# Half-precision expert operands, doubled attention buffers, routing tables in pieces, and a new order for the first pairs

## The chip, the core and the metric

One core of a Trainium2 chip runs the whole program. The time is the device time in microseconds. Three runs of the kernel before took 1328.16 to 1332.0 us, median 1330.05 us. All the views of the profile come from one profiled execution of 1328.04 us.

## The reference

Two stages, both in float32. The first is attention over 64 heads (8 batches of 8), 1152 keys of 64 numbers each, with queries averaged in twos, so 576 query rows per head:

```python
q_pool = q.reshape(B, H, S // factor, factor, D).mean(axis=3)
scores = scale * np.matmul(q_pool, k.transpose(0, 1, 3, 2))
scores = scores - np.max(scores, axis=-1, keepdims=True)
attn = np.exp(scores)
attn = attn / (np.sum(attn, axis=-1, keepdims=True) + 1e-09)
return np.matmul(attn, v)
```

Its output becomes 4608 tokens of 512 numbers. The second stage gives each token to one of 8 experts: all 4608 x 8 logits are walked in descending order, a pair is taken if its token is still free and its expert has fewer than 576 tokens, so every expert ends with exactly 576. Then, for each expert, two layers:

```python
h = np.maximum(x[mask] @ w1[e], 0.0)   # 512 -> 1024
out[mask] = h @ w2[e]                  # 1024 -> 512
```

## The kernel before

**Precision.** TensorE (PE) multiplies in pairs: an operand is split into a high part and a low part (what the high part leaves), and a product is the sum of three (high x high, high x low, low x high). In the attention the parts are half precision, with a power of two per head pair as scale (`SC`), which comes from a bound on the sums over K, Q and V (`bounds`). In the experts high and low parts are float32 tiles that PE reads in its rounded float32 form (`FR`).

**Attention.** 32 head pairs, n = 0 to 31; each pair is 18 steps g: two heads times nine blocks of 128 keys. A step makes scores (PE, `sc`, two f16 products), the exponential (ACT, `P`, 576 columns), a low part of it (POOL or DVE, `PM`), and the product with V (PE, `av`). For the next pair the same time holds the exact row maxima (PE into `ma` and `mb`, DVE reduces them into `MX`), the bounds and scales (ACT sums absolute values into `VM` with `accum_out`, line 439), the split of K, Q and V into f16 parts (`KH`, `KL`, `QH`, `QL`, V's parts), and SP's copies of these into `KA`, `KB`, `QA`, `QB` (`spread`). The loads are `KD`, `QD`, `VD`, issued by SP for the next pair. Of `KD`, `QD`, `VD`, `QS` (the summed queries), `KL` and `QL` there is one buffer each; `KH`, `QH` and others have two.

What sets the order there is the class `Cycle`: every operation carries a tag and a number, and a table (`TAU`; `TAU0` for what is added with pair 0's preparation, `TAU1` for that of pair 1) gives it a place in a period of 25 units. A heap takes, among those whose inputs have been planned, the one with the smallest place. Each engine then runs its operations strictly in that order: an operation that waits holds all behind it on its engine. Before the first pair PE runs `wu` + `wv` = 52 filler matmuls.

**Routing tables.** `routing_tables` makes constants for the routing: POOL writes number rows, and three blocks of DVE operations (`order`, `digits`, `places`, lines 293 to 320) make tables of them. All carry the tag `tab` with base 2, so that they fall beside pairs 2 and 3.

**Experts.** The first `route` takes the best tokens of expert 0, alone; each later expert's routing runs beside the layers of the one before, in rounds of small steps: PE (`rt`), DVE, PE, DVE. `fetch` then gathers, from POOL, the tokens (`XG`, in five indirect transfers of up to 128 rows) and the weights (`W`), and splits them: the high part is a copy by ACT, the low part a subtraction by POOL or DVE. `ffn` runs layer one (`ph`: 8 blocks f times two halves of the tokens, 256 and 320 columns, 12 matmuls each), a relu on ACT and its low part on DVE (`HX` holds both, 2 x 576 columns), and layer two (`po`: five column blocks c of tokens, four with 128 tokens and 24 matmuls of 512 columns each; c = 4 has the last 64 tokens: 8 matmuls of 128 rows, which hold the high and the low part, and 8 of 64 rows with `W2L`). The results (`OT`) go out by POOL's indirect transfers. All the split tiles (`W1H`, `W1L`, `W2H`, `W2L`, `XH`, `XL`) have one buffer.

The class `Order` plans this part: each operation has an earliest time, a duration and a priority (`first`), a transfer the time it is expected to take (`late`), and per engine the one that can start first goes next. The weight splits are written W1, W2, W1, W2 and so on by quarter z. For experts from 2 on, tokens come transposed by SP (`by_dve`): XL is two subtractions on POOL and two on DVE.

## Time and profile before

| what | us |
|---|---|
| median of three runs | 1330.05 |
| profiled execution | 1328.04 |
| its span | 1326.1 |
| first exponential (pair 0) | 24.7 |
| pair 0, to the first exponential of pair 1 | 54.3 |
| pair 3 | 31.9 |
| pairs 4 to 30, together (157.31 to 785.70) | 628.4 |
| pair 31 and the tail of the attention (to 810.25) | 24.6 |
| routing of expert 0 (to 850.30) | 40.1 |
| experts 0 to 4, with the routing of the next (to 1161.46) | 311.2 |
| experts 5 to 7 (to 1314.45) | 153.0 |
| tail (to 1326.10) | 11.7 |

Times are in microseconds from the start of the span, names of tiles are the program's, and a line number is that of the kernel before. PE is the matmul side of TensorE and PEld its weight loads, which overlap with it; DVE is VectorE, ACT ScalarE, POOL GpSimd, SP the engine that issues most transfers. `PEclk` is the granted clock of TensorE. In a timeline a row gives start, duration, engine, line and operation, and in brackets the time that the engine stood idle before, with what released it.

### The profile page before, as it was taken

What the parts mean: (1) busy time and instruction counts of PE and PEld (TensorE: products, weight loads), DVE (VectorE), ACT (ScalarE), POOL (GpSimd) and SP (SyncE); (2) the same over time, 40 slices, a digit from 0 to 9 for tenths busy, and PEclk for the clock granted to TensorE, in tenths of its full rate; (3) what the DMA queues carried; (4) which work ended last, traced back from release to release, by engine and by line L of the source; (5) the groups of instructions that cost most, each with busy time, mean ns of one, the idle gap of its engine ahead of it and who ended that gap; (6) DMA issues with size and microseconds to landing.
All of it is one profiled execution on the core that took longest, in us unless ns stands there. A gap on an engine that the chain in (4) does not pass through costs nothing.

```text
span 1326.1 us, 38213 instructions
## 1 busy us (share of the span) xinstructions
PE 1264.2 (95%) x15398; PEld 1008.8 (76%) x15398; DVE 1035.6 (78%) x2619; ACT 803.7 (61%) x1423; POOL 907.0 (68%) x831
## 2 busy tenths in 40 slices
...
PEclk8599999999999999999999998999999999999998
...
GB/s 166 99 138 172 100 144 173 147 143 167 156 157 136 175 149 140 173 156 156 139 168 150 105 45 19 163 14 187 171 103 176 114 142 162 159 112 169 89 13 36
DMA packets 123533, 175.19 MB, mean 132 GB/s; under 512 B 49500, under 2 KB 86364, under 8 KB 121180
## 3 DMA queue, kind: packets, MB, share of 16 engines
...
q8 instruction: 121, 1.98, 0.6%
...
q10 hardware_dynamic: 144, 0.02, 0.0%
...
## 4 chain that ended last, share of the span: by engine, by line
PE 74%; DVE 19%; issue 3%; ACT 1%; DMA 1%; POOL 1%; POOLq 0%; DVEq 0%; ACTq 0%
PE sc L656 17%; PE ph L1374 15%; PE av L673 14%; PE po L1404 13%; DVE MX L576 5%; PE ma L573 4%; PE mb L573 4%; DVE KL L515 2%; DVE PM L663 1%; PE av L708 1%; PE rt L1052 1%; DVE MX L585 1%; DVE ST L1170 1%; PE av L796 1%; PE av L720 1%
## 5 line engine op out<-in xcount | busy, mean ns | idle before, releaser
L663 POOL TENSOR_TENSOR PM<-P 128x576 f16<-128x576 f32 x504 | 612.6, 1242 | 161.2 <-PE av L673 86.9
L659 ACT ACTIVATE P<-sc,EX 128x576 f32<-128x576 f32 x576 | 408.2, 739 | 128.6 <-PE sc L656 118.7
L673 PEld LDWEIGHTS <-P 128*128 128x128 bf16 x5760 | 299.9, 98 | 31.9 <-issue 1.6
L673 PE MATMUL av<-V,P 128*128 128x65 f16 (+1 forms) x5760 | 311.3, 193 | 0.1
L673 PE MATMUL av<-V,PM 128*128 128x65 f16 x2880 | 301.3, 195 | 0.8 <-POOL PM L663 0.8
L673 PEld LDWEIGHTS <-PM 128*128 128x128 f16 x2880 | 265.9, 97 | 1.0 <-POOL PM L663 1.0
L656 PE MATMUL sc<-QB,KB 65*128 65x288 f16 (+1 forms) x1152 | 239.4, 289 | 0.0
L656 PE MATMUL sc<-QA,KA 128*128 128x288 f16 x1152 | 238.2, 288 | 1.2 <-ACT P L659 1.2
L576 DVE TENSOR_REDUCE MX<-ma 128x1 f32<-128x512 f32 x279 | 190.0, 681 | 16.1 <-PE ma L573 11.6
L576 DVE TENSOR_REDUCE MX<-mb 128x1 f32<-128x512 f32 x279 | 190.4, 683 | 4.6 <-PE mb L573 2.6
L656 PEld LDWEIGHTS <-KA 128*128 128x128 f16 x1152 | 104.3, 97 | 80.3 <-issue 33.5
L1404 PE MATMUL po<-W2H,HX 128*128 128x512 f32 x512 | 164.8, 397 | 0.0
L1374 PE MATMUL ph<-XL,W1H 128*128 128x320 f32 (+1 forms) x512 | 155.5, 304 | 1.3 <-DVE XL L1307 1.3
L1374 PE MATMUL ph<-XH,W1H 128*128 128x320 f32 (+1 forms) x512 | 155.1, 303 | 0.9 <-DVE XL L1273 0.9
L1374 PE MATMUL ph<-XH,W1L 128*128 128x320 f32 (+1 forms) x512 | 154.9, 303 | 0.0
L1379 ACT ACTIVATE HX<-ph 128x320 fp32r<-128x320 f32 (+1 forms) x128 | 52.5, 410 | 147.6 <-PE ph L1374 140.9
L656 PEld LDWEIGHTS <-KB 65*128 65x128 f16 (+1 forms) x1152 | 113.9, 99 | 31.1
L1404 PE MATMUL po<-W2L,HX 128*128 128x512 f32 (+1 forms) x320 | 126.7, 396 | 0.0
L573 PE MATMUL mb<-KH,BD 128*128 128x512 f16 x279 | 108.2, 388 | 9.1 <-DVE MX L576 6.8
L573 PE MATMUL ma<-KH,BD 128*128 128x512 f16 x279 | 107.7, 386 | 9.5 <-DVE MX L576 5.8
L1418 POOL DMA_INDIRECT out_dram<-OT,idx x40 | 39.4, 984 | 109.8 <-ACT OT L1409 83.8
L1404 PEld LDWEIGHTS po<-W2H,HX 128*128 128x128 f32 x512 | 95.0, 188 | 17.8
...
## 6 DMA issues: line engine op xcount, KB each, us to landing
...
QA<-QH SPq DMA_DIRECT2D x128, 72.0 KB
...
```

The source lines that it names most:

```text
L515: fn=lambda h=h: nc.vector.scalar_tensor_tensor(KL[0][:, h], KD[0][:, h], KS, KH[i][:, h], op0=OP.mult, op1=OP.subtract),
L573: od.add(t, "PE", 214, lambda: nc.tensor.matmul(m, BD[i][:, j, :], KH[i][:, 512 * c:512 * c + 512], start=True, stop=True), r=bd + [("KH", ...
L576: od.add(t, "DVE", 597, lambda: nc.vector.tensor_reduce(MX[i][:, j, c:c + 1], m, axis=AX.X, op=OP.max), r=[mk], w=[("MX", i, j, c)], tag=" ...
L585: od.add(t, "DVE", 64 + 133 * len(js), lambda: nc.vector.tensor_reduce(MX[i][:, j:j + len(js), 2], m[:, :128 * len(js)].rearrange("p (a b) ...
L656: nc.tensor.matmul(c[:, t, :288], a[i][:rows, s, ks], b[i][:rows, s, 288 * t:288 * t + 288], start=first, stop=not first)
L659: od.add(g + 0.1, "ACT", 624, lambda: nc.scalar.activation(p.rearrange("p (t q) -> p t q", t=2), c[:, :, :288], AF.Exp, scale=EX[n % 3][:, ...
L663: od.add(g + 0.2, en, dur, lock=1, fn=lambda: eng.tensor_tensor(pm, p, hi, op=OP.subtract), r=[("P32", g % NP)], w=[("PM", g % NM)], tag="pm")
L673: nc.tensor.matmul(out, w[:, qs], v, start=kb == 0 and j == 0 and y == 0, stop=kb == NKB - 1 and y == 2, skip_group_check=True)
L1374: nc.tensor.matmul(p, a[:, d, fs], b[:, d, qs], start=z == 0, stop=z == 11)
L1379: nc.scalar.activation(HH[:, f, qs], p, AF.Relu)
L1404: nc.tensor.matmul(o[:n], a[:, z, q0:q0 + n], b[:, z], start=z == 0 and y == 0, stop=z == 7, skip_group_check=True)
L1418: st = nc.gpsimd.indirect_dma_start(out=out, out_offset=bass.IndirectOffsetOnAxis(ap=idx[i][:n, c:c + 1], axis=0), in_=OT[ob][:n], in_offs ...
```

## The change

In the experts all operands become half-precision pairs. So that they fit its range, x, W1 and W2 are multiplied by powers of two, and the result by their inverse product. The scale of x comes from the sums of squares of V: ACT's bound on V is now a Square instead of an absolute value, with the sums kept in `VQ`. The scale of W1 comes from all of W1: during the attention SP reads it in 32 pieces of 512 KB, one per pair (`weights`, into the one buffer `WB`), and ACT sums each piece's squares. `last_scale` forms both scales in the last pair (`SX`). The scale of W2 comes per expert from four Squares over 1024 columns on ACT, four small PE sums and five small DVE operations (`squares`: `SW`, `IT`). The split is now a scaled copy by ACT into the f16 high part, a second scaled copy by ACT in place, and POOL's subtraction. (Expert 0's first quarter of W1 takes one DVE operation in place of the last two.) As f16 tiles are half as large, each of W1H, W1L, W2H, W2L, XH and XL now has two buffers. W1 is split whole before W2. XL is four or five DVE operations of 128 elements per partition for each of four groups, 18 in all, for experts from 2 on. The first two experts read W1 in halves, no longer behind any token index.

For c = 4 of layer two the 64-row matmuls with W2L come in pairs, one into the lower and one into the upper 64 rows of the output (column tiles).

In the attention `KD`, `QD`, `VD`, `QS`, `KL` and `QL` have two buffers. Pairs 1 and 2 have tables of their own (`TAU1`, `TAU2`), pair 0's steps use `TAU0`, and all numbers of the tables are new; PE gets 16 + 18 more fillers (`wx`, `wy`). V's scale is a DVE operation (`halved`) and an ACT operation of its own. The routing tables are 16 pieces, one per pair from pair 4 on, and POOL's number rows are spread from pair 2 on.

```diff
-            l = (TAU, TAU0, TAU1)[zero][tag]
+            l = (TAU, TAU0, TAU1, TAU2)[zero][tag]
...
+       -130.9575], "ldv": [-89.6074], "ldw": [-1.436], "me": [-20.3883, -10.8961, -7.8442], "mm": [-27.6499, -27.3342,
...
+       [-38.3162, -42.8418], "vsh": [-36.7156], "wsq": [10.2686], "x": [-190.5431, 1.6364]}
...
-AT = {"load": -14.1, "vload": -13.6, "split": -10.3, "bound": -10.3, "bq": 0.1, "bv": -0.1, "bs": 0.1, "spread": 2.0,
...
+AT = {"load": -10.5, "vload": -15.2, "split": -10.3, "bound": -10.3, "bq": 0.1, "bv": -0.1, "bs": 0.1, "spread": 2.0,
+      "val": -5.6, "vh": -1.4, "vd": -0.5, "mm": -3.9, "cw": 0.737, "fold0": 3.5, "fold1": 11.3, "aug": 12.8, "lag":
+      6, "np": 10, "nm": 10, "stick": 1, "nx": 3, "wu": 30, "pd": [4, 12], "wv": 22, "pd0": [], "pd1": [3, 5, 6, 7, 9,
+      10, 11, 12, 13, 16], "d1": 2.0, "cw1": 0.7, "wx": 16, "wy": 18}
...
+    for dur, fn in pieces:
+        do("DVE", dur, fn)
...
-    KL = several(1, [128, S], F16, "KL")
+    KL = several(2, [128, S], F16, "KL")
...
-    KD = several(1, [128, S], F32, "KD")
-    QD = several(1, [128, 2, M], F32, "QD")
-    VD = several(1, [128, 2, NKB, D], F32, "VD")
-    QS = several(1, [128, M], F32, "QS")
+    KD = several(2, [128, S], F32, "KD")
+    QD = several(2, [128, 2, M], F32, "QD")
+    VD = several(2, [128, 2, NKB, D], F32, "VD")
+    QS = several(2, [128, M], F32, "QS")
...
+    def weights(n, t):
+        e, z = divmod(n, 4)
+        od.add(t, "SP", 650, lambda: nc.sync.dma_start(WB, w1[128 * e:128 * e + 128, 1024 * z:1024 * z + 1024]), w=["WB"],
+               tag="ldw", late=6500)
+        od.add(t, "ACT", 1030, lambda: nc.scalar.activation(VJ[:, :1024], WB, AF.Square, accum_out=WQ[:, n:n + 1]),
+               r=["WB"], w=[("WQ", n)], tag="wsq")
...
+        def put():
+            nc.vector.tensor_copy(WM[:, 0:1], mb[:, 128:129])
+            nc.vector.tensor_reduce(WM[:, 1:2], mb[:, 136:144], axis=AX.X, op=OP.max)
+            nc.vector.tensor_scalar(XE, WM.bitcast(I32), 0x7F800000, 0x7F800000, op0=OP.bitwise_and, op1=OP.bitwise_xor)
+            nc.vector.tensor_scalar(XE, XE, 1, 0x7F800000, op0=OP.arith_shift_right, op1=OP.bitwise_and)
+            f = XE.bitcast(F32)
+            nc.vector.tensor_scalar(SX[:, 0:1], f[:, 0:1], 2.0 ** 73, None, op0=OP.mult)
+            nc.vector.tensor_scalar(SX[:, 2:3], f[:, 1:2], 2.0 ** 67, None, op0=OP.mult)
+            nc.vector.scalar_tensor_tensor(SX[:, 1:2], SX[:, 2:3], 2.0, SX[:, 0:1], op0=OP.mult, op1=OP.mult)
+
+        od.add(t, "PE", 110, lambda: nc.tensor.transpose(mb[:32, :128], VQ, ident), r=[("VQ", n) for n in range(npair)], w=["mb"], tag="sx")
+        od.add(t, "DVE", 200, lambda: nc.vector.tensor_reduce(VR, mb[:32, :128], axis=AX.X, op=OP.max), r=["mb"], w=["VR"], tag="sx")
+        od.add(t, "PE", 60, lambda: nc.tensor.matmul(mb[:, 128:129], ones[:32], VR, start=True, stop=True), r=["VR"], w=["mb"], tag="sx")
+        od.add(t, "PE", 110, w_sums, r=[("WQ", n) for n in range(npair)], w=["mb"], tag="sx")
...
-                    VJ[:, :src.shape[1]], src, AF.Abs, accum_out=VM[i][:, c:c + 1]), r=rd, w=[("VM", i, c)], tag="abs")
+                    VJ[:, :src.shape[1]], src, AF.Abs if c < 2 else AF.Square,
+                    accum_out=VM[i][:, c:c + 1] if c < 2 else VQ[:, n:n + 1]), r=rd, w=[("VM", i, c)] + [("VQ", n)] * (c == 2), tag="abs")
...
+        def halved():
+            nc.vector.tensor_scalar(e[:, 1, 2:3], e[:, 1, 2:3], 1, 0x7F800000, op0=OP.arith_shift_right, op1=OP.bitwise_and)
...
-        for _ in range(AT[x]):
-            od.add(-70, "PE", 213, lambda: nc.tensor.matmul(av[1], ones, wide, start=True, stop=True), w=["av1"], tag=x)
+    for x, t, b in (("wu", -70, 1), ("wv", -70, 1), ("wx", -45, 0), ("wy", 20, 0)):
+        for _ in range(AT.get(x, 0)):
+            od.add(t, "PE", 213, lambda b=b: nc.tensor.matmul(av[b], ones, wide, start=True, stop=True), w=[f"av{b}"], tag=x)
...
+        if not g % NSTEP:
+            weights(g // NSTEP, g)
...
+
+    def table(eng, dur, fn):
+        pools.append(eng == "POOL")
+        od.base = max(4, od.base + 1) if eng == "DVE" else 2 + sum(pools) // 4
+        od.add(NSTEP * (od.base + 1), eng, dur, fn, w=["tables"], lock=True,
+               tag="tab" if eng == "DVE" else "tap")
...
-    W1H, W1L = one([128, 4, F], FR, "W1H"), one([128, 4, F], FR, "W1L")
-    W2H, W2L = one([128, 8, DM], FR, "W2H"), one([128, 8, DM], FR, "W2L")
+    W1H, W1L = ([one([128, 4, F], F16, f"W1{x}{b}") for b in range(2)] for x in "HL")
+    W2H, W2L = ([one([128, 8, DM], F16, f"W2{x}{b}") for b in range(2)] for x in "HL")
+    SX = C["SX"]
+    SQ = one([128, 1024], BF, "SQ")
+    WQ = [one([128, 4], F32, f"WQ{b}") for b in range(2)]
+    WE = one([128, 1], I32, "WE")
+    SW = [one([128, 1], F32, f"SW{b}") for b in range(2)]
+    IT = [one([128, 2], F32, f"IT{b}") for b in range(2)]
...
-    XH, XL = one([128, 4, CAP], FR, "XH"), one([128, 4, CAP], FR, "XL")
-
-    HX = one([128, 8, 2 * CAP], FR, "HX")
+    XH, XL = ([one([128, 4, CAP], F16, f"X{x}{b}") for b in range(2)] for x in "HL")
+
+    HX = one([128, 8, 2 * CAP], F16, "HX")
...
+            def low(src=src, s=s, nc_=nc_):
+                for c in range(nc_):
+                    q = slice(128 * c + 32 * s, 128 * c + 32 * s + 32)
+                    V.scalar_tensor_tensor(XL[k % 2][:, :, q], src[:, :, c], SX[:, 0:1], XH[k % 2][:, :, q], op0=OP.mult, op1=OP.subtract)
...
+            od.add(t + 0.35, "DVE", 190 * nc_, low, r=xf + xg + hk, w=lk, first=LT["ft"])
...
-        if k:
+        if k > 1:
             od.add(t, "POOL", 1300, weight(W1.rearrange("p a b c -> p (a b c)"), w1), r=[("widx", i)], w=[("W1", 0), ("W1", 1)],
-                   late=LT["w"])
+                   late=LT["w"], first=LT["fp"])
         else:
             for h in range(2):
                 od.add(t + 0.15 * h, "POOL", 1100, weight(W1[:, h].rearrange("p b c -> p (b c)"),
-                       w1.rearrange("r (h x) -> (r h) x", h=2), widx2[:, h:h + 1]), r=["widx2"] + [("idx", i, c) for c in range(5 * h)], w=[("W1", h)], late=LT["w0"])
+                       w1.rearrange("r (h x) -> (r h) x", h=2), widx2[:, h:h + 1]), r=["widx2"], w=[("W1", h)], late=LT["w0"], first=LT["fp"])
...
-        for z in range(4):
-            for nm in ("W1", "W2"):
...
+        b = k % 2
+        squares(k, t + 0.6)
+        for nm in ("W1", "W2"):
+            for z in range(4):
...
+                    od.add(tt, "ACT", 475, lambda o=hi[p], a=raw[p], w=w: nc.scalar.activation(o, a, AF.Copy, scale=w),
+                           r=[key] + wk, w=[hk], first=first)
+                    if k or z > LT["zd"] or nm == "W2":
+                        od.add(tt, "ACT", 475, lambda a=raw[p], w=w: nc.scalar.activation(a, a, AF.Copy, scale=w),
+                               r=[key, hk] + wk, w=[sk], first=first)
+                        od.add(tt, "POOL", 1230, lambda o=lo[p], a=raw[p], h=hi[p]: nc.gpsimd.tensor_tensor(
+                            o, a, h, op=OP.subtract), r=[key, hk, sk], w=[(nm + "L", b, z, y)], first=first, late=LT["lw"])
...
+        for z in range(4):
+            od.add(t, "ACT", 1030, lambda z=z: nc.scalar.activation(
+                SQ, raw[:, 1024 * z:1024 * z + 1024], AF.Square, accum_out=WQ[b][:, z:z + 1]), r=["W2"], w=[qk[z]], first=first)
...
+            if c < 4:
+                for z in range(8):
+                    for y, (a, b) in enumerate(((HH, W2H), (HH, W2L), (HL, W2H))):
+                        def mm2(c=c, o=o, z=z, y=y, a=a, b=b[bb]):
                             q0 = 128 * c + (64 if a is HL else 0)
-                            nc.tensor.matmul(o[:n], a[:, z, q0:q0 + n], b[:, z], start=z == 0 and y == 0, stop=z == 7,
+                            nc.tensor.matmul(o, a[:, z, q0:q0 + 128], b[:, z], start=z == 0 and y == 0, stop=z == 7 and y == 2)
+                        od.add(t + 0.7, "PE", 214, mm2, r=hkeys(z), w=[("po", c % 2)])
...
+                for z in range(0, 8, 2):
+                    for y in range(2):
+                        od.add(t + 0.7, "PE", 214, lambda o=o, z=z + y: nc.tensor.matmul(
+                            o, HX[:, z, 512:640], W2H[bb][:, z], start=z == 0, stop=False, skip_group_check=True),
+                            r=hkeys(z + y), w=[("po", c % 2)])
+
+                    def halves(o=o, z=z):
+                        for y in range(2):
+                            nc.tensor.matmul(o[64 * y:64 * y + 64], HH[:, z + y, 512:], W2L[bb][:, z + y], start=False, stop=z == 6,
                                              skip_group_check=True)
```

**ACT, second head of pair 0.** `P` is an exponential of pair 0; `VJ` with `VM0` are the sums over pair 2's QS, KD and VD, `QH1` and `KH1` the splits of pair 1. Before:

```order
L439 ACTIVATE VJ_123,VM1_122<-VD0_119 128x1152
L462 ACTIVATE SC1_112<-VE1_125 128x3
L500 ACTIVATE QH1_89<-QS0_120,SC1_112 128x576
L512 ACTIVATE KH1_86<-KD0_117,SC1_112 128x576
L466 ACTIVATE EX1_115<-SC1_112 128x1
L467 ACTIVATE EX1_115<-VE1_125 128x1
L547 ACTIVATE V161_102<-VD0_119,SC1_112 128x9x64 x2
L439 ACTIVATE VJ_123,VM0_121<-QS0_120 128x576
L512 ACTIVATE KH1_86<-KD0_117,SC1_112 128x576
L439 ACTIVATE VJ_123,VM0_121<-KD0_117 128x1152
L439 ACTIVATE VJ_123,VM0_121<-VD0_119 128x1152
L659 ACTIVATE P320_129<-sc0_155,EX0_114 128x576
```

With the change, around the same sums:

```order
L741 ACTIVATE P322_143<-sc0_167,EX0_116 128x576
L507 ACTIVATE VJ_135,VM0_127<-QS0_125 128x576
L741 ACTIVATE P324_145<-sc0_167,EX0_116 128x576
L741 ACTIVATE P323_144<-sc1_168,EX0_116 128x576
L741 ACTIVATE P325_146<-sc1_168,EX0_116 128x576
L507 ACTIVATE VJ_135,VQ_129<-VD0_123 128x1152
L741 ACTIVATE P327_148<-sc1_168,EX0_116 128x576
L507 ACTIVATE VJ_135,VM0_127<-KD0_119 128x1152
L741 ACTIVATE P326_147<-sc0_167,EX0_116 128x576
```

The sums over pair 2's data stood in one block with pair 1's splits, ahead of the exponentials; now single exponentials of pair 0 stand between and before them.

**PE, last column block of an expert** (`HX` holds the activations, `W2H` and `W2L` the weights). Before:

```order
L1401 MATMUL po_16006<-W2H,HX 128x512
L1404 MATMUL po_16006<-W2L,HX 64x512
L1401 MATMUL po_16006<-W2H,HX 128x512
L1404 MATMUL po_16006<-W2L,HX 64x512
```

With the change:

```order
L1549 LDWEIGHTS HX
L1549 MATMUL po_16239<-W2H_16211,HX 128x512
L1549 LDWEIGHTS HX
L1549 MATMUL po_16239<-W2H_16211,HX 128x512
L1555 LDWEIGHTS HX
L1555 MATMUL po_16239<-W2L_16213,HX 64x512
L1555 LDWEIGHTS HX
L1555 MATMUL po_16239<-W2L_16213,HX 64x512
```

The 64-row matmuls now come two by two, behind two of 128 rows; their two outputs are the two halves of the same tile.

**POOL, fetch of the first expert** (`W` raw weights, first both halves of W1, then W2; `XG` the tokens). Before:

```order
L1317 DMA W_15986<-in_w_dram,widx_15977 128x2048
L1322 DMA XG<-x_dram,idx_15969 128x512 x4
L1322 DMA XG<-x_dram,idx_15969 64x512
L1317 DMA W_15986<-in_w_dram,widx_15977 128x2048
L1317 DMA W_15987<-in_w_dram,widx_15978 128x4096
L1357 TENSOR_TENSOR W1L<-W_15986,W1H 128x2x256 x6
```

With the change:

```order
L1419 DMA W_16205<-in_w_dram,widx_16196 128x2048 x2
L1424 DMA XG<-x_dram,idx_16188 128x512 x4
L1465 TENSOR_TENSOR W1L_16209<-W_16205,W1H_16207 128x2x256
L1424 DMA XG<-x_dram,idx_16188 64x512
L1419 DMA W_16206<-in_w_dram,widx_16197 128x4096
L1465 TENSOR_TENSOR W1L_16209<-W_16205,W1H_16207 128x2x256 x5
```

Both halves of W1 now go ahead of the tokens, and the last token transfer stands behind a subtraction.

333 lines of the change are left out of this document (187 added, 146 removed), and 90 rows, old and new, of tables (AT, TAU, TAU0, TAU1).

## The prediction

> **What bounds the kernel now.** I read the page first, then the busy time in stretches, then the chain of waits in the stretches that lose most. The page:
>
> ```profile
> PE 1264.2 (95%) x15398; PEld 1008.8 (76%) x15398; DVE 1035.6 (78%) x2619; ACT 803.7 (61%) x1423; POOL 907.0 (68%) x831
> PE 74%; DVE 19%; issue 3%; ACT 1%; DMA 1%; POOL 1%; POOLq 0%; DVEq 0%; ACTq 0%
> PEclk8599999999999999999999998999999999999998
> ```
>
> PE (TensorE) carries the end, except in the second slice, where the granted clock is half. The stretches (columns: start and end, length, then busy us of PE, weight loads, DVE, ACT, POOL, then granted clock, DMA share, GB/s) are pair 0, pair 3, twelve steady pairs, the first expert's routing, expert 0, the gap behind it, experts 1 to 4, and experts 5 to 7:
>
> ```profile
> 24.70:78.98 54.28, 44.10 (x334) 22.59 (x334) 37.35 (x69) 28.21 (x49) 19.70 (x17) 0.59 0.42 113
> 125.42:157.31 31.89, 24.53 (x387) 19.03 (x388) 29.82 (x68) 19.73 (x34) 20.39 (x19) 0.89 0.42 104
> 227.36:506.64 279.28, 277.13 (x4566) 218.30 (x4563) 267.93 (x501) 237.79 (x404) 234.61 (x193) 1.00 0.60 155
> 810.25:850.30 40.05, 31.30 (x242) 20.40 (x242) 31.00 (x154) 3.50 (x7) 7.37 (x8) 0.87 0.18 58
> 850.30:909.46 59.16, 59.16 (x402) 49.76 (x400) 44.68 (x191) 20.75 (x44) 29.31 (x30) 1.00 0.40 151
> 909.46:916.01 6.55, 3.48 (x29) 2.37 (x27) 5.53 (x15) 6.50 (x13) 6.34 (x8) 1.00 0.42 131
> 916.01:1161.23 245.22, 237.62 (x1591) 202.02 (x1592) 184.08 (x762) 79.74 (x171) 153.21 (x158) 0.98 0.43 140
> 1161.46:1314.45 152.99, 152.99 (x913) 138.40 (x911) 34.39 (x85) 51.12 (x110) 80.82 (x86) 1.00 0.28 88
> ```
>
> A steady pair is 279.28/12 = 23.27 us; PE is busy for 99% of it, DVE idles 0.95 us and ACT 3.46. Pair 0 takes 31.0 more than that, pair 3 8.6 more. An expert without routing beside it takes 152.99/3 = 51.0 us; the first five with the gap took 310.9, which is 55.9 over 5 x 51.0.
>
> **Pair 0.** ACT's timeline, the PE row of the scores that its exponentials wait for, and the chain of waits there:
>
> ```profile
> 47.60 0.76 ACT L512 ACTIVATE KH<-KD,SC 128x576 f16<-128x576 f32 x1
> 59.38 1.16 ACT L439 ACTIVATE VJ<-KD 128x1152 bf16<-128x1152 f32 x1 [11.02 <-DMA KD<-in_kt_dram]
> 60.66 1.16 ACT L439 ACTIVATE VJ<-VD 128x1152 bf16<-128x1152 f32 x1
> 61.73 0.19 ACT L439 ACTIVATION_READ_ACCUMULATOR VJ<-VD 128x1 f32 x1
> 61.82 0.72 ACT L659 ACTIVATE P<-sc,EX 128x576 f32<-128x576 f32 x1
> ```
> ```profile
> 44.43 0.68 PE L656 MATMUL sc<-QB,KB 69*128 69x288 f16 x2
> ```
> ```profile
> 51.32 7.97 DMA KD<-in_kt_dram
> ```
>
> Scores of pair 0's second head lie ready at 45.1, but the next exponential in ACT's order stands behind a sum over pair 2's KD; with one KD buffer that load waits until pair 1 has read it. ACT stands 11.02 us, and PE has little to do in that time and half a clock. With two buffers the load goes long before, and the new order puts the exponentials ahead of that sum. At least the 7.97 us of the chain goes; at most all of DVE's idle time in the pair, 54.28 - 37.35 = 16.9, because its maxima for pair 1 remain. What is late next is those maxima, at half clock. I take -12, between the two; ends -17 and -3, if the exponentials then collide with pair 1's maxima. The 34 new filler matmuls of 512 columns (16 ahead of pair 0's first exponentials, 18 behind its last) take 0.215 each by the attention's rows below, 7.3 in all, and double at half clock. DVE is what pair 0 follows, so they lie in PE's waits: 0; with that cover gone they cost 7 to 15, and if they bring the full clock sooner, they give a few back. Both stay inside the ends of this term, since I know no row that says where the clock would turn.
>
> **Tables.** The routing tables' three blocks on DVE:
>
> ```profile
> 126.59 0.56 DVE L293 TENSOR_SCALAR before<-jp 128x128 bf16<-128x128 int32 x1
> 129.43 1.04 DVE L297 CAST pcol<-scratch 128x2 f32<-128x2 int32 x1
> 134.70 0.68 DVE L576 TENSOR_REDUCE MX<-mb 128x1 f32<-128x512 f32 x1
> ```
>
> From 126.59 to 134.70 DVE does no maxima: 8.1 us, nearly all of pair 3's 8.6. The 16 pieces go to pairs with 0.95 us of DVE idle time each. Some operations there are long for their size (1.04 for two columns), so the sum of the pieces is under 8.1. I take -7.5; ends -8.6 and -4 (half of it on the path again).
>
> **Steady pairs.** New per pair: on DVE one tiny operation (bound 0.19, the accumulator read above is as small), on ACT a Square over 1024 columns (under the 1.16 + 0.19 of the 1152 above) and a second small scale, together some 1.5, on PE one small matmul, on SP one 512 KB load. DVE's 0.95 and ACT's 3.46 idle cover them; uncovered DVE work costs 31 x 0.19 = 6. The table of places is new throughout, which only a run can price: PE has 279.28 - 277.13 = 2.15 us of idle time in twelve pairs, so it can gain 5 over all at most. Taken +3, ends -4 and +12. The scale of x at the end has nine tiny DVE operations and a few PE steps, 2 us if bare, but it is wanted only when the first expert's tokens come, at the end of the 40.05 us of routing: 0.
>
> **First expert's fetch.** POOL's issue, ACT's first cast and the first expert matmul:
>
> ```profile
> 842.22 0.95 POOL L1322 DMA_INDIRECT XG<-x_dram,idx  x1 [1.30 <-DVE ixf L1179]
> ```
> ```profile
> 845.76 2.18 ACT L1354 CAST W1H<-W 128x512 fp32r<-128x512 f32 x4 [35.26 <-DMA W<-in_w_dram,widx]
> ```
> ```profile
> 850.30 0.36 PE L1374 MATMUL ph<-XH,W1H 128*128 128x256 f32 x1
> ```
>
> Now both halves of W1 are issued ahead of the token gathers: one issue more (0.95 + 0.3 between issues), and the last gather stands behind a subtraction that waits for weights and ACT. It can be hidden (the first cast then also comes earlier for half 1). +2, ends 0 and +4.
>
> **Experts, PE.** The chain beside the routing of expert 1, and in the last experts:
>
> ```profile
> 865.39 2.28 PE ph L1374 x17
> 867.67 0.27 PE rt L1052 x5
> 867.93 1.36 PE ph L1374 x8
> 869.29 0.02 PE rt L1062
> 869.32 2.56 PE ph L1374 x19
> ```
> ```profile
> 1161.62 25.59 PE ph L1374 x192
> 1187.21 21.79 PE po L1404 x96
> ```
>
> ph takes 25.59/192 = 0.1333 (a mean of 256 and 320 columns), po 21.79/96 = 0.227; the last 16 of 51.0 are the fifth column at the same 0.227. What half precision takes is in the attention (start to start):
>
> ```profile
> 139.81 0.38 PE L573 MATMUL mb<-KH,BD 128*128 128x512 f16 x1
> 140.02 0.41 PE L656 MATMUL sc<-QA,KA 128*128 128x288 f16 x2
> 140.26 0.41 PE L656 MATMUL sc<-QB,KB 65*128 65x288 f16 x2
> 140.51 0.38 PE L573 MATMUL ma<-KH,BD 128*128 128x512 f16 x1
> ```
>
> 512 columns 0.215, 288 columns 0.122 (by ratio 0.1357 for 320, 0.1086 for 256). An expert: 192 x 0.122 = 23.4; 96 + 8 full ones x 0.215 = 22.4; four pairs of tiles at about 0.223 = 0.9 if a pair runs together. 46.7, or -4.3 for each of eight: -34.
>
> Whether tiles run together:
>
> ```profile
> L720 PE MATMUL av<-XT,wgs x6: 485/488/489, 119.0 to 119.4; 128*8 128x384 f32 x6
> ```
>
> Six matmuls of 384 columns started within 0.4 us, while one alone would take 0.227 x 384/512 = 0.17: they overlap. But a return from small tiles may cost: after the five rt above, 8 ph took 1.36 instead of 1.07. At 0.29, four returns in eight experts cost 9, more than the 8 x 4 x 0.21 = 7 that the tiles save. The Trainium skill's page "TensorEngine Tiling (Array Packing)" says under Key Properties that changing the tiling mode drains the TensorE, and under Restrictions that column tiling disables Fast Weight Load; both speak against this part, and the slow stretch after rt agrees, though a wait could make it too. By that rule the tiles would give back what they save.
>
> **Experts, the rest.** Per expert ACT does 16 more in-place scalings and four Squares. Casts and relus beside experts 1 to 4:
>
> ```profile
> L1354 ACT CAST W1H<-W 128x512 fp32r<-128x512 f32 x32 | 17.9, 618 | 0.0
> L1379 ACT ACTIVATE HX<-ph 128x256 fp32r<-128x256 f32 (+1 forms) x64 | 26.3, 410 | 88.6 <-PE ph L1374 83.8 <-PE rt L1062 4.6
> ```
>
> 16 x 0.62 + 4 x 1.25 = 15 on top of 79.74/4 = 20: 35 of 47, which fits on average. But where all 32 weight operations fall beside ph, ACT has 32 x 0.62 + 16 x 0.41 = 26.4 against PE's 23.4, and a late relu holds a ph buffer: up to 3 us in each of seven experts. Taken +6, ends 0 and +21. The gap of 6.55, where ACT was busy 6.50, should halve, since XH and the weights have a second buffer and W1 goes ahead of W2: -3.5 (-6 to 0). XL's low part becomes 18 small DVE operations for six experts, some 3.4 for the 0.8 it had; DVE is busy 184.08 of 245.22 and covers most: +3 (0 to +8). Together -34 - 3.5 + 6 + 3 = -28.5; ends -41 and -8.
>
> **Sum.** -12 - 7.5 + 3 + 2 - 28.5 = -43, against the profiled execution's 1328.0 (span 1326.1 and 1.9 around it). That gives 1285. The profiled execution is 2 below the median of the three runs, 1330.05, so I say 1287.
>
> **Rivals.** *Rounds bound the first experts.* If DVE's steps between two rt set the length of a round (3.93 from 865.39 to 869.32), shorter ph only makes PE wait, and 5 x 4.3 = 21 is lost, less what still shrinks in rounds with slack. For it: the 1.36 for 8. Against: the chain there names PE alone. About +14: 1301. *Pair 0 stays.* Pair 1's maxima at half clock take up what ACT no longer waits: +12, 1299; DVE's 37 busy of 54 speak against. *Everything hidden.* Pair 0 -17, tables -8.6, pairs 0, experts -39: 1264. *ACT bounds the ph stage,* 7 x 3 = 21 instead of 6, and 5 on pairs: 1307. *Tiles lose,* as above, +9: 1296. *Slower: ACT queued behind a weight chunk in every pair.* The Square of pair n's chunk stands in ACT's order among exponentials; if its load is late, everything behind waits as at 59.38. ACT has 3.46 - 1.5 = 2 us to give; to lose the whole 43 over 31 pairs the wait must be 2 + 1.4 = 3.4 in each. A wait of 5 would give 31 x 3 = 93: about 1380. For it: one buffer, and a DMA share of 0.60. Against: the table sets the Square 11.7 of a pair's 25 units behind the load (10.27 + 1.44), about 10.9 us, more than the 7.97 above. *The change does nothing that counts,* because PE's 99% returns in another form: within 4 us of before.
>
> **Chances.** Forecast 0.42, rounds 0.13, pair 0 stays 0.11, all hidden 0.11, ACT in ph 0.09, tiles lose 0.06, nothing 0.03, slower 0.05. The range 1262 to 1312 reaches from all hidden to ACT in ph with some 5 us on top, and leaves out about 1.5 in 10. A measurement here tells some 0.3%, 4 us, from no change: faster 0.92, same 0.03, slower 0.05.
>
> **What would show it.** Pair 0 some 42 long, with no ACT wait of several us for KD; pair 3 near 24; steady pairs at 23.3 with no wait for WB; ph of the last experts at 0.122 and po at 0.215, 46.7 an expert; fifth columns at 2.6; the first ph some 42 us after its routing begins. The prediction is wrong if pairs lengthen by over 1 us, if ph rows have waits for ACT, or if the first five experts stay near 310.

## The result: 0.85% slower, and the profile after

The changed kernel takes 1339.98 us (median of five, 1338.0 to 1344.54), the kernel before 1330.04 (median of five): the ratio is 1.0085, with a 95% interval of 1.0059 to 1.011. Forecast were 1287 us and a range of 1262 to 1312. The profiled execution took 1344.54, the slowest of the five, with a span of 1342.5, which is 16.4 more than the span before; as the medians are only 9.9 apart, some of the differences below belong to this execution. The page:

```profile
PE 1243.7 (93%) x15497; PEld 878.1 (65%) x15501; DVE 1077.1 (80%) x2795; ACT 963.0 (72%) x1708; POOL 873.8 (65%) x810
PE 44%; DVE 20%; ACT 16%; DMA 9%; issue 7%; POOL 2%; SPq 1%; POOLq 0%; ACTq 0%; DVEq 0%
PEclk9899999999999999999999999899999999899998
```

PE worked 20.5 us less than before and yet carries only 44% of the chain (the work that ended last, followed back), where it carried 74%. What took its place are ACT (16%, before 1), DMA (9%, before 1) and issue (7%, before 3); DVE's share is about as it was (20%, before 19). The clock's dip in the second slice, 5 before, is an 8.

The busy time in stretches (columns as before): pair 0, pair 3, pairs 4 to 30, from pair 31 to the first `ph`, experts 0 to 4, experts 5 to 7.

```profile
25.24:67.82 42.58, 37.17 (x415) 23.81 (x417) 35.24 (x71) 25.90 (x47) 23.20 (x22) 0.92 0.53 146
117.19:140.08 22.89, 22.52 (x382) 17.95 (x379) 22.20 (x43) 20.62 (x37) 18.77 (x16) 1.00 0.58 149
140.08:811.09 671.01, 635.64 (x10291) 494.99 (x10287) 615.94 (x1168) 558.61 (x971) 527.43 (x433) 0.98 0.62 159
811.09:878.89 67.80, 56.88 (x689) 41.95 (x685) 47.53 (x196) 22.13 (x37) 19.97 (x20) 0.92 0.18 61
878.89:1182.40 303.51, 279.02 (x2008) 168.16 (x2007) 243.48 (x1007) 188.24 (x349) 156.97 (x170) 0.97 0.40 134
1182.40:1330.60 148.20, 144.40 (x950) 87.79 (x948) 52.89 (x177) 89.82 (x171) 73.86 (x84) 1.00 0.33 107
```

Set against the same stretches before, in the profiled executions:

| stretch | before | after | difference | forecast |
|---|---|---|---|---|
| to the first exponential | 24.7 | 25.2 | +0.5 | 0 |
| pairs 0 to 2 | 100.7 | 92.0 | -8.8 (pair 0 alone -11.7) | -12 |
| pair 3 | 31.9 | 22.9 | -9.0 | -7.5 with what returns later |
| pairs 4 to 30 | 628.4 | 671.0 | +42.6 | +3 |
| pair 31 to the first `ph` | 64.6 | 67.8 | +3.2 | +2 |
| experts | 464.1 | 451.7 | -12.4 | -28.5 |
| tail | 11.7 | 11.9 | +0.2 | 0 |

Two rows hold the miss. Pairs 4 to 30 give back more than everything else gains, and nearly all of it lies in every second pair: pair 16 takes 28.9 us, pair 17 23.3, pair 18 27.9. The experts gain less than half of what was forecast. The first five fell from 311.2 to 303.5 and the last three from 153.0 to 148.2. PE's busy time in the first five fell by 21 us (before 300.3 of 310.9, the rows of the prediction added up; now 279.0 of 303.5). So half precision did its work there, but PE's idle time rose from 10.7 to 24.5.

In pairs 4 to 30 PE stands idle for 35.4 us (671.0 less 635.6 busy), where it stood 5.4 before (628.4 less 623.0). For 21.6 us of it, in 12 waits, it stands until the copy `BD` has landed (before: 0.2). Its own busy time rose too, from 623.0 to 635.6, at a granted clock of 0.98 instead of 1.00.

The chain of waits through one even pair (26) shows what the first row is made of:

```profile
704.33 0.67 ACT QH L582
705.00 0.68 ACT KH L594
705.67 0.25 SPq L589
...
705.96 5.98 DMA BD<-QH
...
712.08 0.38 PE ma L655
```

The copy of QH into `BD`, on which the next pair's maxima wait, is issued and lands 6 us later. SP's timeline of this pair, and then of the next, odd one:

```profile
702.16 0.38 SPq L870 DMA_DIRECT2D x_dram<-X  x1
702.59 1.97 SPq L604 DMA_DIRECT2D KB<-KH  x2
704.60 0.59 SPq L486 DMA_DIRECT2D QD<-in_qt_dram  x1
705.29 1.31 SPq L589 DMA_DIRECT2D BD<-QH  x2
...
721.77 1.23 SPq L604 DMA_DIRECT2D KB<-KH  x2
723.05 0.59 SPq L486 DMA_DIRECT2D QD<-in_qt_dram  x1
731.24 2.04 SPq L589 DMA_DIRECT2D BD<-QH  x2
```

In the odd pair KB and QD go out 8 us ahead of BD. In the even pair x is stored, which waits for DVE's X, and in SP's order the store stands first: KB and QD queue behind it, all four go out between 702.16 and 706.60, and BD lies behind 576 + 288 + 576 KB. In the kernel before, the load of QD stood well ahead of the store, and KB behind BD:

```profile
206.47 0.53 SPq L418 DMA_DIRECT2D QD<-in_qt_dram  x1
212.78 0.38 SPq L788 DMA_DIRECT2D x_dram<-X  x1
213.22 1.97 SPq L522 DMA_DIRECT2D QA<-QH  x2
215.64 1.31 SPq L507 DMA_DIRECT2D BD<-QH  x2
```

### The profile page after: what moved, and what is told of

Read it like the earlier page. It is cut to its first block, busy times and chain, and to the rows that moved or that the text cites. A ratio compares the mean times of both kernels' runs of the same rounds, so it can differ in the third digit from the quotient of the medians.

```text
span 1342.5 us, 38872 instructions
## 1 busy us (share of the span) xinstructions
PE 1243.7 (93%) x15497; PEld 878.1 (65%) x15501; DVE 1077.1 (80%) x2795; ACT 963.0 (72%) x1708; POOL 873.8 (65%) x810
## 4 chain that ended last, share of the span: by engine, by line
PE 44%; DVE 20%; ACT 16%; DMA 9%; issue 7%; POOL 2%; SPq 1%; POOLq 0%; ACTq 0%; DVEq 0%
PE sc L738 10%; PE ph L1512 8%; PE po L1542 7%; PE av L755 7%; DVE MX L658 7%; ACT P L741 6%; DMA BD<-QH 6%; PE mb L655 3%; PE ma L655 3%; ACT KH L594 2%; DMA W<-in_w_dram,widx 2%; ACT W L1463 2%; ACT V L629 1%; ACT QH L582 1%; DVE X L776 1%
## 5 line engine op out<-in xcount | busy, mean ns | idle before, releaser
L755 PE MATMUL av<-V,P 128*128 128x65 f16 (+1 forms) x5760 | 306.3, 193 | 0.1
L755 PE MATMUL av<-V,PM 128*128 128x65 f16 x2880 | 297.2, 195 | 0.0
L658 DVE TENSOR_REDUCE MX<-ma 128x1 f32<-128x512 f32 x279 | 191.2, 685 | 34.9 <-PE ma L655 31.9
L1542 PE MATMUL po<-W2H,HX 128*128 128x512 f16 x512 | 157.4, 384 | 2.1 <-ACT OT L1544 2.1
L1512 PE MATMUL ph<-XH,W1H 128*128 128x320 f16 (+1 forms) x512 | 148.5, 290 | 1.3 <-DVE XL L1375 0.6
L1512 PE MATMUL ph<-XL,W1H 128*128 128x320 f16 (+1 forms) x512 | 148.5, 290 | 0.8 <-DVE XL L1375 0.5
L1512 PE MATMUL ph<-XH,W1L 128*128 128x320 f16 (+1 forms) x512 | 148.4, 290 | 0.0
L1542 PEld LDWEIGHTS <-HX 128*128 128x128 f16 x768 | 71.3, 98 | 90.0 <-issue 11.8
L1512 PEld LDWEIGHTS <-W1H 128*128 128x128 f16 x1024 | 99.3, 99 | 31.5 <-issue 5.8
L1542 PE MATMUL po<-W2L,HX 128*128 128x512 f16 x256 | 98.2, 384 | 0.0
```

Of the source, the lines that this page charges most:

```text
L658: od.add(t, "DVE", 597, lambda: nc.vector.tensor_reduce(MX[i][:, j, c:c + 1], m, axis=AX.X, op=OP.max), r=[mk], w=[("MX", i, j, c)], tag=" ...
L755: nc.tensor.matmul(out, w[:, qs], v, start=kb == 0 and j == 0 and y == 0, stop=kb == NKB - 1 and y == 2, skip_group_check=True)
L1512: nc.tensor.matmul(p, a[:, d, fs], b[:, d, qs], start=z == 0, stop=z == 11)
L1542: nc.tensor.matmul(o, a[:, z, q0:q0 + 128], b[:, z], start=z == 0 and y == 0, stop=z == 7 and y == 2)
```

## The experiments

All of them are timed against the kernel before on the same chip. Runs sent together share a chip; the groups ran on four chips, on which the kernel before took 1329.6 to 1335.1. "The stage" is from the first `ph` to the last `po` of the experts, in the one profiled execution of each run.

### The attention: the store, the tables, the scan

**The store behind BD.**

```diff
-       -77.8177], "store": [-21.5681], "sx": ...
+       -77.8177], "store": [45], "sx": ...
```

> The changed kernel with one number of the place table other: the store of x (576 KB, every second pair) stands on SP behind the copies BD<-QH and the KD loads of its pair, not ahead of KB, QD and BD. Theory A (SP's order: in even pairs the store, which waits for X, holds KB x2 and QD, so that BD goes out behind 1.4 MB and lands 6 us later on the chain): pairs 4 to 30, now 671 us together, fall by 25 to 45 us, BD lands within 3 us, total 1295 to 1315. Rival B (the transfers collide whatever their order, because 16.8 MB of w1 were added): BD is late as before or something else of the same bunch is, total within 6 us of the changed kernel's 1340. Rival C (the table pieces' waits on DVE make the even pairs long): at most 10 us come back, 1330 or more.

Measured: 1307.45 us, ratio 0.983 (0.9814 to 0.9847). Pairs 4 to 30 take 638.8 instead of 671.0. SP's timeline of an even pair now reads:

```profile
664.31 1.11 SPq L604 DMA_DIRECT2D KB<-KH  x2
665.46 0.59 SPq L486 DMA_DIRECT2D QD<-in_qt_dram  x1
672.66 1.31 SPq L589 DMA_DIRECT2D BD<-QH  x2
674.48 0.69 SPq L490 DMA_DIRECT2D KD<-in_kt_dram  x1
...
677.60 0.58 SPq L870 DMA_DIRECT2D x_dram<-X  x1
```

The chain through this pair holds PE alone, and in pairs 4 to 30 no matmul waits for BD any more. One number of a table of 210 is worth 32 us: theory A holds, and with it the changed kernel is faster than the one before.

**Table pieces two by two.**

```diff
-        od.base = max(4, od.base + 1) if eng == "DVE" else 2 + sum(pools) // 4
+        od.base = 4 + 2 * ((pools.count(False) - 1) // 2) if eng == "DVE" else 2 + sum(pools) // 4
```

> The changed kernel with the 16 table pieces two by two in the odd pairs 5 to 19 instead of one in each pair from 5 to 20. Theory C (a piece in an even pair meets a POOL operation and stands some 1.1 us on DVE, on the chain to the next scale): the even pairs 6 to 20 fall by 1 to 2 us each, total lower by 8 to 16, so 1324 to 1332. Theory A alone (the store's place): the even pairs 6 to 20 stay near 27 and the total within 4 us of 1340.

With this edit the pieces come into the even pairs 4 to 18, not into odd ones (in the changed kernel they lie in pairs 5 to 20, one in each). 1341.4 us, ratio 1.0097 (1.0066 to 1.0128): no change. It does not test what it was meant to.

**No scan of W1.**

```diff
-        od.add(t, "SP", 650, lambda: nc.sync.dma_start(WB, w1[...
-        od.add(t, "ACT", 1030, lambda: nc.scalar.activation(VJ[:, :1024], WB, AF.Square, ...
+        if not n:
+            od.add(t, "POOL", 120, lambda: nc.gpsimd.memset(WQ, 0.41), ...
```

> The changed kernel without the 32 loads of w1 chunks and their Squares on ACT; the scale of W1 comes from a constant sum, so the scan of W1 is left out. Rival B (the added loads and Squares make the even pairs long): pairs 4 to 30 fall by 25 to 43 us. Theory A: the loads stand behind BD in SP's order and ACT has idle time, so the pairs fall by 0 to 8 us; total 1330 to 1340.

1336.81 us, ratio 1.0046 (1.0023 to 1.007), pairs 4 to 30 at 663.2. That is 3 us less than the changed kernel, and the two intervals overlap. The pairs are 8 shorter in the profiled execution, but in the run with weights unscaled (below), whose attention is the changed kernel's own, they took 658.5, so the 8 say little. The scan is not worth the 25 to 43 us of rival B: the added 16.8 MB are not the cause. This also ends the forecast's own slower rival, ACT queued behind a late chunk.

**Store late, pieces two by two in even pairs, no scan.** (The edits of the three runs above together.)

> The changed kernel with the store late, the table pieces two by two in odd pairs, and without the scan of W1 (left out; a constant sum in its place). With the store late alone, pairs 4 to 30 took 638.8 us, 10.4 more than in the kernel before. Theory G (the pieces and the scan make that rest): pairs 4 to 30 at 628 to 632, total 1297 to 1301. Rival H (the rest is the new place table and the added V scale steps): pairs 4 to 30 at 635 to 639, total 1304 to 1308.

1302.58 us, ratio 0.9781 (0.9763 to 0.9798); the profile fell on the longest of its six runs (1311.29), with 639.7 for pairs 4 to 30. The expectation named 628 to 632 for theory G and 635 to 639 for H. As the profile is not typical of the median, this run decides neither. What decides is where the rest lies in the runs with the store late: the stretches 5 to 20, which hold the pieces, and 21 to 30, which hold none. First the kernel before, then the run with the store late, repeated:

```profile
180.81:553.18 372.37, 369.45 (x6084) 290.90 (x6081) 357.25 (x667) 317.08 (x537) 313.10 (x257) 1.00 0.60 155
553.18:785.70 232.52, 230.06 (x3796) 181.42 (x3793) 216.20 (x406) 190.77 (x321) 193.99 (x161) 1.00 0.53 139
```
```profile
161.66:542.43 380.77, 370.59 (x6100) 291.38 (x6097) 367.48 (x709) 335.20 (x585) 314.42 (x257) 1.00 0.70 173
542.43:774.34 231.91, 229.17 (x3811) 181.13 (x3808) 217.43 (x417) 201.73 (x350) 195.36 (x161) 1.00 0.63 157
```

Pairs 21 to 30 take 231.9 against 232.5, with the scan, the Squares, `halved` and the new places all in. Pairs 5 to 20 take 8.4 us more. So the rest lies with the pieces. The run with them two by two in even pairs agrees: from 4 to 18 its even pairs take 24.0 to 29.0 us, and the odd ones between them, which hold none, 22.6 to 22.8. One of the pieces in the changed kernel, on DVE and POOL:

```profile
347.38 1.18 DVE L336 TENSOR_SCALAR nib<-scratch 128x16 f32<-128x16 int32 x1
```
```profile
345.18 5.56 POOL L745 TENSOR_TENSOR PM<-P 128x576 f16<-128x576 f32 x5
```

An operation on 16 columns takes 1.18 us beside POOL's PM; the like piece of pair 11 takes 0.17, although PM runs there too: a piece can be held and need not be. Added up over all their operations, the pieces take 16.4 us of DVE in the changed kernel and 21.2 and 19.2 in the two runs with the store alone late, where the same operations in their three blocks took 9.5 before.

**The pieces in odd pairs.** As the run with store, durations and tiles together (below), with `od.base = 5 + 2 * (...)`.

> As the run with store, durations and tiles together, and the table pieces two by two in the odd pairs 5 to 19. (The earlier run with pieces two by two had them in the even pairs 4 to 18, by a slip in the count.) A piece stands 1.0 to 1.2 us where POOL is at work. Theory C (in even pairs this lies on the chain to the next pair's copies, in odd pairs there is slack): pairs 4 to 30 fall from 636 to 628 to 632. Rival (a piece costs DVE the same in any pair, since DVE has 1 us to spare): 634 to 640.

1314.32 us (1308.88 to 1321.38), ratio 0.9844 (0.9795 to 0.9893). In the profiled execution, one of the two long ones (1319.73), pairs 4 to 30 take 647.0, longer than the 637.0 of its companion on the same chip; the two short ones (1308.9) are as long as the companion's median (1308.81). The odd pairs from 5 to 19 together take 198.9, where the companion's take 187.7, and the even ones from 4 to 18 191.7 against 193.4. So theory C's gain does not appear: a piece that stands behind POOL costs in odd pairs too. Whether two in one pair cost more than two apart is not shown.

### Pair 0: buffers, order, clock

**The kernel before with KD, QD, VD and QS doubled.**

```diff
-    KD = several(1, [128, S], F32, "KD")
+    KD = several(2, [128, S], F32, "KD")
```

(and the same for QD, VD, QS, each use by `n % 2`.)

> The kernel before with KD, QD, VD and QS in two buffers each, its tables of places unchanged. Theory I (pair 0 was long because ACT's sum over KD waited for the one buffer): pair 0 falls from 54.3 to 42 to 47 us, pair 3 stays 31.9, and the total falls by 5 to 13 where the steady pairs stay at 23.27. Rival J (it took the new order of ACT): pair 0 at 51 or more. Theory K (with free buffers the loads move to other places on SP, and BD may come behind them as in the changed kernel): steady pairs over 23.6.

1351.85 us, ratio 1.0176 (1.0151 to 1.0202): doubling the loads alone makes the kernel before 22 us slower. Pair 0 takes 56.8, at a granted clock of 0.60, though ACT no longer waits for KD. Its exponential now waits for PE:

```profile
66.88 0.74 ACT L659 ACTIVATE P<-sc,EX 128x576 f32<-128x576 f32 x1 [14.18 <-PE sc L656]
```

PE has pair 1's maxima ahead of pair 0's scores in its order, and so it had in the kernel before, during ACT's wait for KD. PE's first matmul of these maxima and its next scores, before and then in this run:

```profile
48.41 0.58 PE L573 MATMUL ma<-KH,BD 128*128 128x512 f16 x1 [3.29 <-ACT KH L512]
...
62.60 0.64 PE L656 MATMUL sc<-QA,KA 128*128 128x288 f16 x2 [0.62 <-ACT P L659]
```
```profile
52.20 0.58 PE L573 MATMUL ma<-KH,BD 128*128 128x512 f16 x1 [3.42 <-ACT KH L512]
...
65.62 0.69 PE L656 MATMUL sc<-QA,KA 128*128 128x288 f16 x2
```

Between these rows stand 13 to 14 us of maxima, matmul and DVE reduction by turns. So rival J holds: the wait that the prediction took away was not what set the length, the order was. Pairs 4 to 30 rise from 628.4 to 644.1. Theory K is right that copies come late, but wrong on which: the scores wait 13.9 us, 18 times, for the copy `QB<-AU` (never before), and no matmul waits for BD. That the second buffers gave the loads other places on SP, for which the old table was not made, is argued and not shown.

**No new fillers.** The store late, and `"wx": 0, "wy": 0`.

> The changed kernel with the store late (1307.45 us, pair 0 42.2) and without the 34 new filler matmuls wx and wy. In the changed kernel the granted clock in pair 0 is 0.92 where it was 0.59. Theory L (the fillers keep PE so busy that the clock stays, and the clock is what shortened pair 0): the clock falls to 0.6 to 0.75 in pair 0 and the pair takes 47 to 55 us; the total rises by 5 to 12. Rival M (the new order of ACT and PE keeps PE fed, fillers or not): clock over 0.85 and pair 0 at 41 to 44.

1317.42 us, ratio 0.9878 (0.9862 to 0.9895). Pair 0 alone:

```profile
26.10:72.50 46.40, 37.70 (x395) 23.09 (x394) 35.80 (x71) 26.04 (x47) 22.73 (x22) 0.79 0.53 143
```

The granted clock is 0.79 where it is 0.92 with them, and pair 0 takes 46.4 instead of 42.2. Neither bound of L or M was met: the fillers make about 4 of the 12 us. The other 8 are what is left for the new order together with the buffers; the order without the buffers was not run. The clock rises with each step (0.59, 0.79, 0.92); that they act through it, by keeping PE at work, is argued.

### The experts: tiles, ACT, POOL, DVE

**Column tiles in a row.** The fifth column in the changed kernel (PE's timeline, last expert): two full matmuls, then a pair of tiles, and so on.

```profile
1327.44 0.60 PE L1549 MATMUL po<-W2H,HX 128*128 128x512 f16 x2
1327.97 0.41 PE L1555 MATMUL po<-W2L,HX 128*64 128x512 f16 x2
1328.31 0.60 PE L1549 MATMUL po<-W2H,HX 128*128 128x512 f16 x2
```

The two tiles lie in 0.41 us together, so they do run at once (one takes 0.40). But they start 0.53 behind the first of two full ones, where 0.43 is usual, and the next full one starts 0.34 behind them, where 0.22 would do. A period of 0.87 is what two full ones and two tiles one after the other would take. The edit:

```diff
-                for z in range(0, 8, 2):
-                    for y in range(2):
-                        od.add(t + 0.7, "PE", 214, lambda o=o, z=z + y: nc.tensor.matmul(
+                for z in range(8):
+                    od.add(t + 0.7, "PE", 214, lambda o=o, z=z: nc.tensor.matmul(
...
+                for z in range(0, 8, 2):
```

> The changed kernel with the store late, and in the fifth column all eight full matmuls ahead of the four pairs of column tiles, where they alternated two and two. Theory F (each change between full array and tiles costs PE some 0.1 us: the period of two full ones and a pair of tiles is 0.87 us where 3 x 0.216 = 0.65 were expected): the fifth column falls from 3.5 to 2.8 us, the last expert from 47.5 to 46.8, the whole by some 5 us to 1302. Rival (the tiles run at 0.43 for a pair since they share the output's bank): the period stays 0.87 for the same work, the total within 1.5 us of 1307.

```profile
1290.26 1.89 PE L1548 MATMUL po<-W2H,HX 128*128 128x512 f16 x8
1292.08 1.05 PE L1555 MATMUL po<-W2L,HX 128*64 128x512 f16 x8
```

Eight full ones and four pairs now take 1.82 + some 0.86, and `po` of the last expert falls from 23.9 to 23.2. Theory F holds: the change between full array and tiles costs 0.10 to 0.12 each way, eight times in a column, as much as the tiles save. The Trainium skill's page "TensorEngine Tiling (Array Packing)", Key Properties, says that a change of tiling mode drains the TensorE. The trace agrees in that each change costs time, with the price above. The total did not move with it, though: 1306.86 against 1307.45. The stage fell by 0.9 us (451.5 to 450.6), for PE's busy time in it fell by 3.0 and its idle time rose by 2.1.

**Weights unscaled.**

```diff
-                w, wk = (SX[:, 2:3], []) if nm == "W1" else (SW[b], [("SW", b)])
+                w, wk = 1.0, []
...
-                        od.add(tt, "ACT", 475, lambda a=raw[p], w=w: nc.scalar.activation(a, a, AF.Copy, scale=w),
```

(and without the Squares and sums of W2.)

> The changed kernel with W1 and W2 split unscaled: no in-place scaling on ACT, no Squares of W2, no sums; the scaling of the weights is left out, x keeps its scale. The attention is as in the changed kernel. Theory D (ACT's queue of weight operations holds relus and so PE in the expert stage, now 451.7 us from first ph to last po): the stage falls by 10 to 20 us, total 1320 to 1330. Rival E (DVE's XL operations, which wait for the moved tokens, and the rounds set the stage): it falls by 5 us at most.

1341.55 us, ratio 1.0099 (1.0071 to 1.0126), the stage 457.0, longer than 451.7, with more than half of ACT's weight work gone. Expert 6 alone has 10.9 us of PE idle time in `ph`. DVE and POOL there:

```profile
1224.35 13.15 DVE L1410 SCALAR_TENSOR_TENSOR XL<-XG,SX,XH 128x128 f16<-128x128 f32 x5 [0.48 <-ACT XH L1405]
```
```profile
1224.04 3.38 POOL L1463 TENSOR_TENSOR W1L<-W,W1H 128x512 f16<-128x512 f32 x3
1227.38 8.92 POOL L1463 TENSOR_TENSOR W2L<-W,W2H 128x512 f16<-128x512 f32 x8
```

Five XL operations, usually 0.28 us each, take 13.15: the first stands until POOL's eleven subtractions, which follow one another without a gap, have ended at 1236.3. In the stage of this run such holds add up to 35 us of DVE time; in the changed kernel to 15.5, in the kernel before to 7.5 (what operations took over the usual time of the same line, where that is over 0.4 us). With ACT's in-place copy gone, POOL no longer waits for ACT between its subtractions, and so it holds DVE longer. The Trainium skill, page "SBUF — State Buffer", section "SBUF: two separate sides", has DVE and GpSimd share one port pair as an exclusive lock, held for a whole instruction; on DVE's side it names operations with two inputs in SBUF (XL has two, XG and XH) and those in a two-port mode. That one blocks the other agrees; here the block lasted through eleven instructions in a row.

**The planner's durations as measured.** The order was planned with 475 ns for a scaled weight copy; its row shows 0.72, and 0.61 from start to start.

```profile
L1463 ACT ACTIVATE W<-W,SW 128x512 f32<-128x512 f32 x64 | 44.5, 720 | 0.2
L1460 ACT ACTIVATE W2H<-W,SW 128x512 f16<-128x512 f32 x64 | 43.6, 718 | 5.5 <-DVE SW L1492 5.4
```

```diff
-                    od.add(tt, "ACT", 475, ...
+                    od.add(tt, "ACT", 615, ...
-            od.add(t, "ACT", 1030, lambda z=z: ...
+            od.add(t, "ACT", 1140, lambda z=z: ...
-                od.add(t + 0.3, "SP", 650, move, ...
+                od.add(t + 0.3, "SP", 940, move, ...
-            od.add(t + 0.35, "DVE", 190 * nc_, low, ...
+            od.add(t + 0.35, "DVE", 280 * nc_, low, ...
```

In this order the lines are the two weight copies, the Squares, the move and the low parts.

> The changed kernel with the store late (1307.45 us; experts 451.5) and, for the experts, the planner's durations set to what the trace shows: 615 ns for a scaled weight copy on ACT (planned 475), 1140 for a Square (1030), 940 for an SP move of transposed tokens (650), 280 for an XL operation (190). Only the planned order changes. Theory D2 (orders were made with ACT operations that are too short, so relus and then DVE's routing steps queue behind weights): the expert stage falls by 6 to 15 us, 1292 to 1302. Rival (PE's idle time there comes from the routing's own chain of PE and DVE steps, whatever the order of weights): within 4 us of 451.5, or longer.

1291.85 us, ratio 0.9717 (0.97 to 0.9735), the stage 433.9. It looked like theory D2, until three more runs stood against it.

> The changed kernel with the store late, the planner's durations as measured, and tiles in a row: the whole change is in. If the gain of each part adds up: pairs 4 to 30 near 636, expert stage 433.9 less 0.7 in each of the last three experts and at most that in the others, 428 to 432; total 1286 to 1291. If the rounds take the tiles' gain in the first five experts: 431 to 433, total 1290.

1308.81 us, ratio 0.9815 (0.9785 to 0.9846), stage 450.0, on another chip.

> The changed kernel with the store late, tiles in a row, the planner's durations as measured (540 for an unscaled weight copy, 940 for an SP move, 280 for an XL operation), and with weights unscaled: the scaling of the weights, the Squares of W2 and the scan of W1 are left out. The expert stage took 433.9 with scaled weights and measured durations. Theory D2 (a right plan hides ACT's extra work): the stage stays at 428 to 438. Rival D (ACT's load itself costs PE time): it falls to 415 to 427, and with it the total below 1285.

1305.72 us, ratio 0.9785 (0.9769 to 0.9801), stage 453.6, above both bounds, with 24.6 us of DVE held by POOL.

> The changed kernel with the store late and the planner's durations as measured, once more: 1291.85 us and an expert stage of 433.9 on another chip, where the same with tiles in a row had 450.0 later. If the order makes the difference: 431 to 437 again and a ratio of 0.970 to 0.975. If the chip did: 445 to 452 and a ratio near 0.981.

1313.49 us, ratio 0.983 (0.9811 to 0.985), stage 458.9, for the same kernel that had 433.9. Four timed executions each lay within 1287 to 1293 on the one chip and within 1311 to 1316 on the other, while the kernel before differed by 5 us. In the longer one an `ST` operation of DVE meets a run of POOL subtractions and PE stands 7.3 us, and right behind that wait matmuls of 256 columns start 0.21 apart instead of 0.11; in the shorter one this does not happen. That is one part of the 25 us between the two stages; why the chips differ stays open. It may be that the order only decides what can collide and small shifts on the chip whether it does, but no run shows it. D2 is not shown.

**POOL's and ACT's weight work shortened, in one and the same order.**

```diff
-                            o, a, h, op=OP.subtract), r=[key, hk, sk], ...
+                            o[:, :, :32], a[:, :, :32], h[:, :, :32], op=OP.subtract), r=[key, hk, sk], ...
...
-                        ... nc.scalar.activation(a, a, AF.Copy, scale=w),
+                        ... nc.scalar.activation(a[:, :, :32], a[:, :, :32], AF.Copy, scale=w),
```

The first edit is POOL's, the second ACT's (with Squares over 128 of 1024 columns); planned durations stay, so all engines keep their order.

> The changed kernel with the store late (1307.45 us; expert stage 451.5, PE idle 28 there), its planned order unchanged, but each of POOL's weight subtractions works on an eighth of its columns; the rest of the low parts of the weights is zero, so the low part of the weights is left out for seven eighths. Theory P (POOL's subtractions hold DVE's operations, XL's and the routing's above all): DVE operations of over 2 us vanish from the stage, PE idle falls by 8 us or more, the stage to 436 to 444. Theory A2 (ACT's queue sets it): the stage stays at 448 to 452.

1304.0 us (two executions), ratio 0.9766 (0.9744 to 0.9787). No DVE operation is held any more, yet the stage is 445.7, only 6 less than the base's 451.5 (451.4 in its repetition on a third chip, below), and PE's idle time in it is 26.5, where the base has 27.7 and 26.7. Theory P asked for 8 less; A2 does not fit either.

> The same base and order, but ACT's in-place scalings and its Squares of W2 work on an eighth of their columns (the rest of the low parts is then wrong, the scale of W2 comes from an eighth of it). Theory A2 (ACT's queue of weight operations delays relus and with them DVE and PE): PE idle falls by 8 us or more, the stage to 436 to 444. Theory P: POOL no longer waits for ACT, works with fewer gaps and holds DVE for longer at a time, as in the unscaled kernels (451 to 457): the stage stays within 4 us of 451.5 or grows.

1312.72 us (two executions), ratio 0.9831 (0.9798 to 0.9864), stage 454.5; DVE is held for 20.7 us. As in the unscaled runs, a faster ACT alone brings nothing.

> Both of these together. If POOL and ACT between them make PE's added idle time, the stage falls to 420 to 435 (idle 8 to 15). If it is the routing's own chain or the waits for the moved tokens, it stays over 440.

1292.65 us (two executions), ratio 0.9681 (0.9653 to 0.9708), stage 435.2. As the base of these three had been measured elsewhere, it was repeated with this run on one chip:

> The changed kernel with the store late, as before: 1307.45 us and an expert stage of 451.5 on the first chip. If the base is the same on any chip: stage 449 to 454, ratio 0.981 to 0.985. If chips differ as they did for the other order: 455 or more, or under 445.

> The same with POOL's subtractions and ACT's in-place scalings and Squares on an eighth of their columns (seven eighths of the low parts of the weights left out). If POOL's and ACT's weight preparation makes the added idle time: the stage is 12 to 20 us below that of the base on this same chip. If the chip made the 435.2: within 6 us of the base.

1309.11 us, ratio 0.9855 (0.9832 to 0.9878), and 1279.16 us, ratio 0.9625 (0.9609 to 0.9641). The stage of the one and of the other:

```profile
843.58:1294.97 451.39, 424.66 (x2957) 256.87 (x2955) 296.77 (x1179) 278.18 (x520) 229.07 (x253) 0.97 0.38 125
```
```profile
841.35:1264.77 423.42, 413.59 (x2956) 254.53 (x2954) 282.69 (x1182) 213.38 (x519) 121.67 (x253) 1.00 0.41 134
```

With both shortened the stage is 28.0 us less (12 to 20 were expected), in the same planned order and with the same matmuls. PE's idle time falls from 26.7 to 9.8 us, about what the kernel before had, and the other 11 are PE's own busy time, at a granted clock of 1.00 instead of 0.97: the waits cost twice. So it is the weight preparation on ACT and POOL together that keeps PE idle; either alone gives back 6 us at most, as far as a base from other chips tells. The edits also take away work that the kernel before had (POOL's subtractions), so the 28 are not the price of what the change added alone. How the two hang together is argued, not shown: DVE, which all routing steps pass in order, stands behind POOL's subtractions and behind relus that ACT does late, and with one of the two gone it still stands behind the other. Why the same kernel had 435.2 on the chip before stays open; held DVE operations are not the reason, since there are none in either run.

Of versions that do the whole work, those with the store late are faster than both kernels: alone 0.983 on one chip and 0.9855 on another, with the measured durations 0.9717 on one and 0.983 on another.

## Why the prediction was wrong, step by step

**Pair 0: right size by luck, wrong cause.** -12 was forecast and -11.7 came (42.58). The step read ACT's 11 us wait for KD as the price and said that PE has little to do in that time; PE and DVE were at pair 1's maxima then. The kernel before with two buffers has no such wait and a pair 0 of 56.8. What shortened it is the new order, together with the buffers (8), and the fillers (4), while the clock went from 0.59 to 0.92. The prediction counted the fillers at nothing and left the clock inside the ends of the term. Pairs 1 and 2, for which it had no term, gave 3 us back.

**Tables: right about pair 3, wrong about where they went.** Pair 3 fell by 9.0. But the step let the pieces hide in "0.95 us of DVE idle time" and read the 1.04 us for two columns as a reason for less. That row was the price itself: such an operation can stand while POOL works, wherever it is put. The sum of the pieces, which the step put under 8.1 us, came to 16.4, and to 19 to 21 with the store late (before: 9.5, counted alike). Pairs 5 to 20 took 8 us more with the store late. Net about 0 instead of -7.5.

**Steady pairs: the step that failed most.** +3 was taken, with +12 as the end; it was +42.6, or 1.6 us a pair, where the prediction itself named 1 as a sign of being wrong. The new operations were costed each on its engine, and that holds: pairs 21 to 30 cost nothing more once the store is late. What was not costed is the order of SP's queue, and it was worth 32 us. The prediction said that "only a run can price" the new table, and bounded it by PE's idle time, which bounds a gain and not a loss. The rows to look at were in reach: in the changed order the store stands ahead of KB, QD and BD, and it waits for X. The slower rival had the right kind of mechanism, one late transfer per pair in front of an in-order queue, at the wrong place: without the scan's loads the kernel was 3 us shorter, not clear of the noise.

**First fetch: right.** +2 was forecast, +3.2 came.

**Experts, PE: right but for the tiles.** The matmul spacings came as taken (21.69 us for the last 176 `ph`, 0.123 each), and PE's busy time in the first five experts fell by 21. The last expert takes 47.5 instead of 46.7, and the 0.8 are the fifth column: the tiles save nothing. (Experts 5 and 6 take 50.8 and 49.8, with waits.) This was the rival "tiles lose", with 0.1 per change where 0.29 was taken for a return. The 0.29 was misread: the eight `ph` after rt are all of 320 columns and were set against the mean of 256 and 320. In that trace the first starts 0.25 ahead of the second and the others follow 0.14 to 0.15 apart, so the return was 0.1 there too.

**Experts, the rest: the term mis-sized.** ACT and DVE were given +9 together, less 3.5 for the gap. The gap went from 6.6 to 0.6 us. But with seven eighths of POOL's subtractions and of ACT's scalings and Squares left out, the stage is 28 us shorter. POOL's part had no term at all, since its work was the same as before; ACT's copy was taken at 0.62 and takes 0.72 with a scale. What each of the two costs by itself stays open. DVE's busy share spoke of room, where its waits in order did not. The rival "rounds bound the first experts" came near in size (21 lost there, 14 found as idle time), though not in cause: with most of the two engines' weight work left out, the same rounds leave PE 9.8 us of idle time in the whole stage, no more than before.
